# A transformer block on one core: the first stage put in another order, with wider dummy matmuls and earlier 256-column FFN blocks

## The chip, the core and the metric

The kernel runs on one core of a Trainium2 chip. The metric is the device time of one execution in microseconds (us). The core has a matrix engine (TensorE, PE in the profile; its weight loads are shown as PEld), a vector engine (DVE), a scalar engine (ACT), a general engine (POOL) and a queue engine (SP), which here issues nearly all DMA transfers. Each engine works through its own instructions in order and waits on semaphores for the others.

## The reference

The input x has 2048 rows of 448 columns, in bf16. It is normalized row by row. Two branches read the normalized rows: a linear attention with 16 heads of width 28 and a two-layer FFN of width 1792. Their results are added to x.

```python
xn  = layernorm(x)
q, k, v = split(xn @ wqkv)                     # 16 heads, width 28
pq, pk  = q @ w_phi, k @ w_phi                 # per head, 28x28
phi(p)  = concat(softmax(p), softmax(-p))      # width 56
num = phi(pq) @ (phi(pk).T @ v)
den = phi(pq) @ sum_s phi(pk) + 1e-6
A   = (num / den) @ wo
B   = silu(xn @ w1) @ w2
out = x + A + B
```

## The kernel before

The rows are worked on in 8 pairs of 128-row tiles. The kernel records every operation with the tiles that it reads and writes, an assumed duration and a priority, and `_Prog.schedule` then lays them out, engine by engine, with a planner of its own. The planner assumes when each load lands: SP issues one load every 550 ns, the bytes flow at up to 290 GB/s (150 GB/s for a transfer into 64 partitions, marked `half`), and a landing follows 1.7 us later. The order found is fixed at build time; semaphores then make each engine wait for what it needs. So the planner's figures decide the order and nothing else.

The work falls into stages:

- *First stage.* SP loads x pair by pair and w1 in column blocks. Dummy matmuls on a zeroed tile `zz` (L545, named "warm") fill PE until the first transposes. `ln_pair(p)` takes the row statistics on DVE (L611, L615), the power -0.5 on POOL (`rstd`, L622), and writes the normalized rows `xn_sb` (L635, on DVE; for pairs 4 to 7 the second tile on POOL). `ln_tr` brings them to column-major order in `xnT`: for pairs 0 to 3 by seven PE transposes (L504) and a copy out of PSUM ("eviction", on ACT for pair 0 at L650, on DVE for the others at L652), for pairs 4 to 7 by a transposing DMA (L556).
- `ffn1_chunk(p0, npair, fa, fb)` multiplies `npair` pairs with the feature tiles `fa` to `fb` of w1 (14 in all), 128 x npair columns to a matmul, and ACT applies SiLU into `hT`. Two PSUM units of two banks each are used in turn. The contraction of 448 goes as 7 steps of 64 rows on both halves of the array, so each weight must lie in both halves of the partitions: `load_main` and `load_tail` load it once, and `swap` copies it across (ACT L511 or DVE L576, one half each).
- `fold()` multiplies the transposed query and key weights `wT` (brought by eight transposing DMAs, L597, "wT_dt") with the per-head matrix of `w_phi` and writes the folded weights, key ones first, into `W_sb`, which lies in the tile `ar`; they are swapped too, and so are the value weights (columns `VO` to `WC`).
- *Key stage.* `k_macro(p)` projects keys and values of a pair, ACT takes the exponentials (L511), DVE copies the values (L773) and forms row sums `Sk` (L778) and reciprocals `Rk` (L780), and POOL multiplies (`phik`, L781). `k_acc` accumulates the key-value product on PE, `q_group` projects the queries.
- *Last stage.* FFN1 of pairs 4 to 7, the query side, FFN2 with w2, the output projection with wo, and the stores. `late_loads` brings w2 and wo; they wait for the exponentials of a pair (the key "early").

The order of recording in the first stage is this (the priorities are equal, so it also breaks ties):

```python
        ln_pair(0)
        swap(w1_sb, 0, 256, ("act", "act"))
        swap(w1_sb, 256, 512, ("act", "act"))
        ffn1_chunk(0, 1, 0, 4)
        ln_pair(1)
        swap(w1_sb, 512, 1024, ("act", "dve"))
        ffn1_chunk(0, 1, 4, 8)
        ffn1_chunk(1, 1, 0, 8)
```

Feature tiles 8 to 13 follow later for pairs 0 to 3 together, 512 columns to a matmul.

Of the kernel before, what the change touches and what calls it, by code (L numbers as in the profile page):

```python
# [144 lines left out]
class _Prog:  # L145
# [72 lines left out]
    def schedule(self):  # L218
# [28 lines left out]
        plan = {}  # L247
        loads = {e: [[o.id, o.nbytes, 0.0] for o in ops if o.is_dma and o.eng == e and not o.deps] for e in ("sp", "act")}
        for e, t0, per in (("sp", -100.0, 550.0), ("act", 1500.0, 600.0)):
            for i, q in enumerate(loads[e]):  # L250
                q[2] = t0 + per * (i + 1)
        now = 0.0
        while loads["sp"] or loads["act"]:
            live = [e for e in ("sp", "act") if loads[e] and loads[e][0][2] <= now]
            nxt = [loads[e][0][2] for e in ("sp", "act") if loads[e] and loads[e][0][2] > now]
            if not live:
                now = min(nxt)
                continue
            cap = [150.0 if ops[loads[e][0][0]].half else 290.0 for e in live]
            rates = [min(c, 290.0 * c / sum(cap)) for c in cap]  # L260
            step = min(min(loads[e][0][1] / r for e, r in zip(live, rates)), min(nxt) - now if nxt else 1e18)
            now += step
            for e, r in zip(live, rates):
                q = loads[e][0]
                q[1] -= step * r
                if q[1] <= 1.0:
                    plan[q[0]] = now + 1700.0
                    loads[e].pop(0)
# [92 lines left out]
def bass_parallel_sum__linear_kernel_hedgehog__dense_activation_silu__prompt_kernel(  # L361
# [20 lines left out]
    with es:  # L382
        def sb(name, shape, dt):
            return es.enter_context(nc.sbuf_tensor(name, shape, dt))
# [153 lines left out]
        P.cur_prio = 0  # L538
        table_op = act(mtmp[:, 0:1], ones4[:, 0:1], ACTF.Silu, "table", table="silu")
        P.cur_prio = 3  # L540
        NWARM = 46
        zz = sb("zz", [128, 256], BF16)
        P.op("dve", 300, lambda e: e.memset(zz[:], 0.0), writes=[zz[:]], name="zz")
        for i in range(NWARM):
            mm(banks[5][:, 0:256], zz[:, 0:128], zz[:, 0:256], True, True, "warm")  # L545
            P.ops[-1].dur = 215.0 if i < 26 else 110.0
        P.cur_prio = 0

        def load(dst, src, nbytes, name, eng="sp", keys_r=(), half=False):
# [8 lines left out]
        def load_x(p0, p1, eng="sp"):  # L558
            load(x_sb[:, 2 * p0:2 * p1, :].rearrange("p (q t) d -> p q t d", t=2), xt[:, p0:p1], (p1 - p0) * 256 * D * 2, f"x{p0}", eng)
# [17 lines left out]

        load_x(0, 1)
        load_main(w1_sb, B_w1, 0, 256, 0, "w1_0")
        load_tail(w1_sb[:, 6], B_w1, 0, 1024, 0, "w1_0t", "act")  # L580
        load_x(1, 2)
        load_main(w1_sb, B_w1, 256, 512, 256, "w1_0b")
        load_x(2, 3)
        load_main(w1_sb, B_w1, 512, 1024, 512, "w1_1")
        load_x(3, 4)
        if not 1:
            load_main(wraw, A_wqkv, 0, 2 * D, 0, "wqk")
            load_tail(wraw[:, 3], A_wqkv, 0, 2 * D, 0, "wqkt")
        load(Wp[:], A_w_phi.rearrange("(g hl) d f -> (hl d) g f", g=G), H * DH * DH * 2, "wphi")
        load_main(w1_sb, B_w1, 1024, FF, 1024, "w1_2")  # L590
        load_tail(w1_sb[:, 6], B_w1, 1024, FF, 1024, "w1_2t")
        load_x(4, 6)
        load_x(6, 8)
        if 1:
            for a in (4, 5, 6, 7, 0, 1, 2, 3):
                dst, src = wT[:, a:a + 1, 0:D], A_wqkv[:, a * KP:a * KP + 128]
                P.dma(lambda e, dst=dst, src=src: e.dma_start_transpose(out=dst, in_=src), 2 * D * 128 * 2, writes=[dst],  # L597
                      name="wT_dt", dur=700.0)
        load_main(W_sb, A_wqkv, 2 * D, 3 * D, VO, "wv")
        load_tail(W_sb[:, 6], A_wqkv, 2 * D, 3 * D, VO, "wvt")  # L600

        def late_loads():
            load(w2_sb[:], B_w2.rearrange("(f p) d -> p f d", p=128), FF * D * 2, "w2", keys_r=("early",))
            for k in range(3):
                load(wo_sb[:, k, :], A_wo[128 * k:128 * k + 128, :], 128 * D * 2, "wo", keys_r=("early",))
            load_tail(wo_sb[:, 6], A_wo, 0, D, 0, "wot")

        BK_F = [4, 7]
        first_xn = []
        def ln_stats(t):  # L610
            o = P.op("dve", 630, lambda e: e.bn_stats(st6[:, t, :], x_sb[:, t, :]),  # L611
                     reads=[x_sb[:, t, :]], writes=[st6[:, t, :]], name="bnst")
            if t >= 2:
                o.odeps |= {q.id for q in first_xn}
            P.op("dve", 180, lambda e: e.bn_aggr(mv[:, t, :], st6[:, t, :]),  # L615
                 reads=[st6[:, t, :]], writes=[mv[:, t, :]], name="bnag")

# [23 lines left out]
        def ln_tr(p, bk):  # L641
            sl = p % NXN
            dstx = xnT[:, :, p, :]
            if p >= 4:
                transpose_dma(dstx, xn_sb[:, sl, :], "xnT_dt")
                return
            tp = bank16[bk][:, 0:896].rearrange("p (j c) -> p j c", j=KB)
            transpose_many([(tp[:, j, :], xn_sb[:, sl, 128 * j:128 * j + 128]) for j in range(KB)], "xnT_tr")
            if p == 0:
                act(dstx, tp, ACTF.Identity, "xnT_ev")  # L650
                return
            P.op("dve", d_dve(896, 2), lambda e: e.tensor_copy(dstx, tp), reads=[tp], writes=[dstx], name="xnT_ev")  # L652

        def ln_pair(p):
            t0, t1 = 2 * p, 2 * p + 1
# [18 lines left out]
        def ffn1_chunk(p0, npair, fa=0, fb=FT, late=False):  # L674
            n = npair * 128
            F = 512 // n
            for f0 in range(fa, fb, F):
                w = min(F, fb - f0)
                b0 = UNITS[unit_no[0] % len(UNITS)]
                unit_no[0] += 1  # L680
                for i in range(w):
                    mm_448([banks[b0 + h][:, i * n:(i + 1) * n] for h in range(2)],
                           lambda h, k, ft=f0 + i: w1_sb[:, k, ft * 128:ft * 128 + 128],
                           lambda h, k: xnT[:, k, p0:p0 + npair, :].rearrange("p a c -> p (a c)"),
                           i == 0, True, "ffn1_mm")
                src = psum[:, b0 * 512:(b0 + 2) * 512].rearrange("p (r c) -> p r c", r=2)[:, :, 0:w * n]
                if w == 1:
                    dst = hT(f0, f0 + 1, 0, 2, p0, p0 + npair).rearrange("p f r a c -> p (f r) (a c)")
                else:
                    src = src.rearrange("p r (f c) -> p r f c", f=w)  # L690
                    dst = hT(f0, f0 + w, 0, 2, p0, p0 + npair).rearrange("p f r a c -> p r f (a c)")
                o = act(dst, src, ACTF.Silu, "silu", table="silu")
                if late:
                    lates.append(o)
                    for q in exps:
                        if q.id not in o.deps:
                            o.odeps.add(q.id)
                else:
                    silus.append(o)
# [8 lines left out]
        def fold():  # L708
# [2 lines left out]
                bd4, Wp[:, :, None, :].broadcast_to([KP, G, 4, DH]),  # L711
                maskh[:, None, :, None].broadcast_to([KP, G, 4, DH]), ALU.mult),
                reads=[Wp[:], maskh[:]], writes=[BDphi[:]], name="bdphi")
            if 1:
                for a in (4, 0):
                    src, dst = wT[0:KP, a:a + 4, 384:448], wT[0:KP, a:a + 4, 448:512]
                    P.op("dve", 230, lambda e, dst=dst, src=src: e.tensor_copy(dst, src), reads=[src], writes=[dst], name="wT_dup")
            for a0 in range(0, 0 if 1 else 8, 4):
                tps = [bank16[b][0:KP].rearrange("p (a c) -> p a c", a=2) for b in BK_F]
                transpose_many([(tps[i // 2][:, i % 2, kt * 128:kt * 128 + 128], wraw[:, kt, (a0 + i) * KP:(a0 + i + 1) * KP])  # L720
                                for i in range(4) for kt in range(4)], "wT_tr")
                for i in range(2):
                    act(wT[0:KP, a0 + 2 * i:a0 + 2 * i + 2], tps[i], ACTF.Identity, "wT_ev")
            for qk in (1, 0):
                for k0 in range(0, 4, 2):
                    parts = []
# [14 lines left out]
        swap(w1_sb, 256, 512, ("act", "act"))  # L741
        ffn1_chunk(0, 1, 0, 4)
        ln_pair(1)
        swap(w1_sb, 512, 1024, ("act", "dve"))
        ffn1_chunk(0, 1, 4, 8)
        ffn1_chunk(1, 1, 0, 8)
        ln_pair(2)
        ln_pair(3)
        fold()
        ffn1_chunk(2, 1, 0, 8)  # L750
        ffn1_chunk(3, 1, 0, 8)
        ln_pair(4)
        swap(w1_sb, 1024, FF, ("act", "dve"))
        ln_pair(5)
        ffn1_chunk(0, 4, 8, FT)
        ln_pair(6)
        ln_pair(7)
        swap(W_sb, VO, WC, ("dve", "dve"))

        def k_unit(p, j, b0, name):  # L760
            mm_448([banks[b0 + t][:, 0:D] for t in range(2)], lambda h, k: xnT[:, k, p, :],
# [49 lines left out]
                 writes=[vaug[:, sl, :, :, DH]], name="vaug1")  # L811
        for p in range(NPAIR):
            k_macro(p)
            if p == 1:
                P.keyw["early"] = exps[-1].id
                late_loads()
            q_group(p // 4, p % 4)
            if p in (2, 4, 6):
                k_acc(p - 2, p)
# [275 lines left out]
```

## Time and profile before

| | |
|---|---|
| median of three runs | 162.54 us (161.03 to 163.39) |
| profiled execution: its time | 159.93 us |
| its span, first to last instruction | 158.2 us |
| granted TensorE clock | 1.000 |
| PE busy | 151.5 us (96%), 2687 matmuls |
| DVE, ACT, POOL busy | 101.4, 75.0, 65.0 us |
| DMA | 12.10 MB in 22905 packets |
| first real matmul, first key projection | 9.84 us, 38.62 us |

Busy time is summed over an engine's instructions. The chain that ended last goes back from the last instruction, at each step to whatever released it; a step named "issue" is time for which the profile shows nothing that was waited for. In a timeline row the first number is the start, the second the length of a group of instructions, then the engine, the line, the operation, out <- in with its shape, the count, and in brackets the idle time before it and what ended it.

### The profile page before, as it was taken

To read this page: it belongs to the slowest core of one execution; us is meant where nothing else is said; L and a number is where in the kernel's file an instruction comes from. 1 tells how busy PE (TensorE), PEld (TensorE's weight loads), DVE (VectorE), ACT (ScalarE), POOL (GpSimd) and SP (SyncE) were. 2 spreads that over 40 slices of the span, in tenths; PEclk is the share of its full clock that TensorE was granted. 3 is DMA by queue.
4 is the path that set the end of the run, shared out by engine and by line. 5 is a ranking of instruction groups with operands and counts; after the bars stand their busy time and mean duration, and the time that the engine had idled before them with its cause. 6 is when DMAs were issued, how large, how long until landed. Compare 5 with 4: busy or idle time off the path is not lost.

```text
span 158.2 us, 5909 instructions
## 1 busy us (share of the span) xinstructions
PE 151.5 (96%) x2687; PEld 97.1 (61%) x2687; DVE 101.4 (64%) x194; ACT 75.0 (47%) x81; POOL 65.0 (41%) x73
## 2 busy tenths in 40 slices
PE   7979699999999999999999999999999999999994
PEld 5777588644444645446778889755555555556553
DVE  5887579884478869688468796667985950022041
ACT  3689267876988878587775665830000000000000
POOL 5221209788046776767900533664166051000000
PEclk9999999999999999999999999999999999999999
DMA  4999883572207900000000023030440044041011
GB/s 120 263 328 261 152 109 94 62 62 58 58 4 198 298 1 6 4 0 4 6 4 4 4 58 62 12 50 4 116 117 6 4 116 116 4 116 58 4 58 58
DMA packets 22905, 12.10 MB, mean 77 GB/s; under 512 B 16096, under 2 KB 22752, under 8 KB 22880
## 3 DMA queue, kind: packets, MB, share of 16 engines
q1 hardware_dynamic: 22720, 11.47, 32.9%
q8 instruction: 21, 0.34, 1.0%
q10 hardware_dynamic: 160, 0.26, 0.6%
q14 instruction: 4, 0.03, 0.1%
HBM read 6.22 MB, written 1.84 MB: 51 GB/s over the span
## 4 chain that ended last, share of the span: by engine, by line
PE 89%; DMA 3%; issue 3%; ACT 2%; SPq 1%; DVE 0%
PE psum L486 85%; PE psum L479 4%; DMA w_sb<-in_B_w_dram 3%; ACT w_sb L511 1%; PE psum L504 1%; SPq L550 1%; ACT ar L511 1%; ACT xnT L511 1%; DVE out_sb L933 0%; ACT L511 0%
## 5 line engine op out<-in xcount | busy, mean ns | idle before, releaser
L486 PE MATMUL psum<-xnT,w_sb 64*128 64x128 bf16 (+2 forms) x924 | 46.0, 253 | 3.3 <-issue 2.2
L486 PEld LDWEIGHTS psum<-xnT,w_sb 64*128 64x128 bf16 x924 | 35.3, 94 | 11.9 <-issue 2.7
L511 ACT ACTIVATE ar<-psum 128x896 bf16<-128x896 f32 (+2 forms) x38 | 32.0, 880 | 10.7 <-PE psum L486 10.6
L889 POOL TENSOR_TENSOR scr<-scr 128x384 bf16<-128x384 f32 (+3 forms) x32 | 20.1, 659 | 31.5 <-DVE scr L884 20.6
L781 POOL TENSOR_TENSOR ar<-ar,Rk 128x1792 bf16<-128x1792 bf16 (+1 forms) x9 | 25.8, 2876 | 14.3 <-DVE Rk L780 12.0
L933 DVE TENSOR_TENSOR out_sb<-psum,x_sb 128x448 bf16<-128x448 f32 (+2 forms) x17 | 9.5, 593 | 23.7 <-PE psum L486 20.5
L486 PE MATMUL psum<-ar,xnT 64*128 64x448 bf16 x224 | 22.7, 349 | 0.0
L486 PE MATMUL psum<-w_sb,hT_lo 64*128 64x448 bf16 x224 | 22.3, 349 | 0.0
L511 ACT ACTIVATE eq<-psum 128x1024 bf16<-128x1024 f32 x16 | 15.5, 1025 | 6.1 <-PE psum L486 6.0
L511 ACT ACTIVATE hT_lo<-psum 128x1024 bf16<-128x1024 f32 x14 | 14.3, 1022 | 7.9 <-PE psum L486 7.9
L778 DVE TENSOR_REDUCE Sk<-ar 128x64 f32<-128x1792 bf16 (+1 forms) x9 | 16.2, 1804 | 2.5 <-ACT ar L511 2.5
L486 PEld LDWEIGHTS psum<-ar,xnT 64*128 64x128 bf16 x224 | 10.8, 94 | 10.6 <-DVE ar L773 0.4
L884 DVE TENSOR_TENSOR scr<-psum,Gq 128x896 f32<-128x896 f32 x16 | 16.9, 1087 | 0.4
L486 PE MATMUL psum<-w_sb,ar 64*128 64x448 bf16 x168 | 16.6, 349 | 0.0
L486 PEld LDWEIGHTS psum<-w_sb,hT_lo 64*128 64x128 bf16 x224 | 10.5, 94 | 9.4
L622 POOL TENSOR_TENSOR rstd<-ve,neghalf 128x2 f32<-128x2 f32 (+1 forms) x9 | 7.1, 792 | 18.6 <-DVE ve L620 16.4
L486 PE MATMUL psum<-xnT,ar 64*128 64x512 bf16 x112 | 13.4, 376 | 0.0
L773 DVE CAST ar<-psum 128x896 bf16<-128x896 f32 x8 | 8.6, 1070 | 7.4 <-PE psum L486 7.4
L486 PEld LDWEIGHTS psum<-w_sb,ar 64*128 64x128 bf16 x168 | 8.4, 94 | 7.4
L486 PE MATMUL psum<-wo_sb,scr 64*128 64x448 bf16 (+2 forms) x119 | 11.9, 338 | 0.0
L635 POOL TENSOR_SCALAR xn_sb<-x_sb,mv,rstd 128x192 bf16<-128x192 bf16 (+1 forms) x8 | 9.9, 1241 | 0.7 <-POOL rstd L622 0.4
L611 DVE BATCH_NORM_STATS2 st<-x_sb 128x6 f32<-128x448 bf16 x16 | 9.6, 612 | 0.1
(51 smaller groups left out, 122.2 us busy)
## 6 DMA issues: line engine op xcount, KB each, us to landing
w_sb<-in_B_w_dram SPq DMA_DIRECT2D x1, 1568.0 KB, 7.8
out_dram<-out_sb SPq DMA_DIRECT2D x7, 224.0 KB, 2.2
x_sb<-in_A_x_dram SPq DMA_DIRECT2D x4, 224.0 KB, 5.0
x_sb<-in_A_x_dram SPq DMA_DIRECT2D x2, 448.0 KB, 8.0
w_sb<-in_B_w_dram SPq DMA_DIRECT2D x1, 576.0 KB, 7.0
w_sb<-in_B_w_dram SPq DMA_DIRECT2D x2, 192.0 KB, 3.8
w_sb<-in_B_w_dram SPq DMA_DIRECT2D x1, 384.0 KB, 5.9
ar<-in_A_wqkv_dram SPq DMA_DIRECT2D x1, 336.0 KB, 3.5
```

Source lines behind the costliest of these rows:

```text
L479: lambda e: e.matmul(dst, lhsT, rhs, start=start, stop=stop, skip_group_check=True),
L486: r = e.matmul(dst, lhsT, rhs, start=start, stop=stop, skip_group_check=True)
L511: return P.op("act", d_act(_cols(src)), lambda e: e.activation(dst, src, func, scale=scale), reads=[src], writes=[dst], table=table, name= ...
L611: o = P.op("dve", 630, lambda e: e.bn_stats(st6[:, t, :], x_sb[:, t, :]), reads=[x_sb[:, t, :]], writes=[st6[:, t, :]], name="bnst")
L622: P.op("pool", 580, lambda e: e.tensor_tensor(r2, v2, nh, ALU.pow), reads=[v2, nh], writes=[r2], name="rstd")
L635: o = P.op("pool" if pool else "dve", 150 + _cols(xs) * 1.6 if pool else 120 + _cols(xs) * 0.6, lambda e, xn=xn, xs=xs: e.tensor_scalar(xn ...
L773: P.op("dve", d_dve(896), lambda e: e.tensor_copy(dstv, vb), reads=[vb], writes=[dstv], name="v_ev")
L778: P.op("dve", d_dve(896 * n), lambda e, S3=S3, E3=E3: e.tensor_reduce(S3, E3, AXL.X, ALU.add), reads=[E3], writes=[S3], name="Sk")
L781: P.op("pool", d_pool(896 * n, 1.77), lambda e, E3=E3, R3=R3, n=n: e.tensor_tensor(E3, E3, R3[:, :, None].broadcast_to([128, 32 * n, DH]), ...
L884: P.op("dve", d_dve(896), lambda e, dsto=dsto, Us=Us, Gs=Gs: e.tensor_tensor(dsto, Us, Gs[:, :, :, :, None].broadcast_to([128, 2, 2, 8, DH ...
L889: P.op("pool", d_pool(_cols(a0), 2.26), lambda e, dst=dst, a0=a0, a1=a1: e.tensor_tensor(dst, a0, a1, ALU.add), reads=[a0, a1], writes=[ds ...
L933: P.op("dve", d_dve(c1 - c0), lambda e: e.tensor_tensor(dst, ob, xs, ALU.add), reads=[ob, xs], writes=[dst], name="out_ev")
```

## The change

- The 31 + 15 dummies of 256 columns become 18 of 512 columns and 10 of 256; `zz` grows to 512 columns and is zeroed in two steps. In the order found, 18 stand before the first transposes, 9 after them and 1 later.
- Pair 0 is evicted by DVE (L652's form) and no longer by ACT. DVE's statistics of the second tile follow the first tile's instead of standing beside them; later statistics are held behind the evictions of pairs 0 and 1.
- w1 comes in another order: columns 512 to 1024, the last 64 rows of columns 512 to 1792, and columns 1024 to 1408 and 1408 to 1792 now stand ahead of x of pairs 2 and 3. The two loads on ACT's queue carry 512 instead of 1024 columns each. The swaps are cut in the same way.
- Feature tiles 8 to 13 are computed for pairs 0 and 1 right after the first block, and for pairs 2 and 3 among the fold's matmuls, with 256 columns each.
- The eight transposing loads of the query and key weights stand ahead of x of pairs 4 to 7, and so behind 12 transfers instead of 13.
- The value weights' swap is recorded in `fold()`, and in the order found stands between the key swaps and the query swaps; the statistics of pair 4 stand ahead of these on DVE.
- w2 is loaded in parts of 4, 3, 4 and 3 feature tiles, released by the exponentials of pairs 1 to 4, and wo by those of pair 5.
- The planner's assumed rates change (310 and 190 GB/s, 1.5 us for a transposing load, one stop of 0.9 us).

```diff
-            cap = [150.0 if ops[loads[e][0][0]].half else 290.0 for e in live]
-            rates = [min(c, 290.0 * c / sum(cap)) for c in cap]
+            cap = [190.0 if ops[loads[e][0][0]].half or ops[loads[e][0][0]].name == "wT_dt" else 310.0 for e in live]
+            rates = [min(c, 310.0 * c / sum(cap)) for c in cap]
...
-        for i in range(NWARM):
-            mm(banks[5][:, 0:256], zz[:, 0:128], zz[:, 0:256], True, True, "warm")
+        for n, rows, cols, dur in ((8, 128, 512, 430.0), (10, 128, 512, 215.0), (10, 128, 256, 109.0)):
+            for i in range(n):
+                mm(banks[5][0:rows, 0:cols], zz[:, 0:rows], zz[:, 0:cols], True, True, "warm")
...
         load_main(w1_sb, B_w1, 0, 256, 0, "w1_0")
-        load_tail(w1_sb[:, 6], B_w1, 0, 1024, 0, "w1_0t", "act")
+        load_tail(w1_sb[:, 6], B_w1, 0, 512, 0, "w1_0t", "act")
         load_x(1, 2)
         load_main(w1_sb, B_w1, 256, 512, 256, "w1_0b")
+        load_main(w1_sb, B_w1, 512, 1024, 512, "w1_1")
+        load_tail(w1_sb[:, 6], B_w1, 512, FF, 512, "w1_1t")
+        load_main(w1_sb, B_w1, 1024, 1408, 1024, "w1_2a")
+        load_main(w1_sb, B_w1, 1408, FF, 1408, "w1_2b")
         load_x(2, 3)
-        load_main(w1_sb, B_w1, 512, 1024, 512, "w1_1")
         load_x(3, 4)
         load(Wp[:], ...)
-        load_main(w1_sb, B_w1, 1024, FF, 1024, "w1_2")
-        load_tail(w1_sb[:, 6], B_w1, 1024, FF, 1024, "w1_2t")
-        load_x(4, 6)
-        load_x(6, 8)
             for a in (4, 5, 6, 7, 0, 1, 2, 3):
                 ...
+        load_x(4, 6)
+        load_x(6, 8)
...
-            if p == 0:
-                act(dstx, tp, ACTF.Identity, "xnT_ev")
-                return
-            P.op("dve", d_dve(896, 2), lambda e: e.tensor_copy(dstx, tp), reads=[tp], writes=[dstx], name="xnT_ev")
+            o = P.op("dve", d_dve(896, 2), lambda e: e.tensor_copy(dstx, tp), reads=[tp], writes=[dstx], name="xnT_ev")
...
-        swap(w1_sb, 512, 1024, ("act", "dve"))
+        swap(w1_sb, 512, 768, ("act", "dve"))
+        swap(w1_sb, 768, 1024, ("act", "dve"))
         ffn1_chunk(0, 1, 4, 8)
+        swap(w1_sb, 1024, 1408, ("act", "dve"))
+        swap(w1_sb, 1408, FF, ("act", "dve"))
+        ffn1_chunk(0, 2, 8, FT)
+        ln_pair(2)
         ffn1_chunk(1, 1, 0, 8)
-        ln_pair(2)
         ln_pair(3)
         fold()
         ffn1_chunk(2, 1, 0, 8)
+        ln_pair(4)
+        ffn1_chunk(2, 2, 8, FT)
         ffn1_chunk(3, 1, 0, 8)
-        ln_pair(4)
-        swap(w1_sb, 1024, FF, ("act", "dve"))
         ln_pair(5)
-        ffn1_chunk(0, 4, 8, FT)
         ln_pair(6)
         ln_pair(7)
-        swap(W_sb, VO, WC, ("dve", "dve"))
```

## The prediction

> **What bounds the kernel now.** I read the page first (engines, slices), then the chain that ended last in order of time, then the timeline of the first 55 us. TensorE (PE) is busy 96% of the span, so the question is only where it is not. The chain in order of time (start us, length us, what) answers that:
>
> ```profile
> 9.84 2.52 PE psum L486 x84
> ...
> 13.96 1.50 PE psum L486 x49
> 15.46 1.79 issue
> ...
> 21.43 0.36 issue
> ...
> 26.55 51.29 PE psum L486 x969
> ...
> 80.58 69.89 PE psum L486 x1096
> ```
>
> From 26.55 us on the chain is PE work but for 2.7 us around 79 us, in which PE itself idles only 0.3. So a change to the first stage pays only by starting the first real matmul (9.84) earlier, by taking out the idle 1.79 and 0.36 us, or by bringing the first key projection forward; and the gain lasts only if the later stage can follow. The timeline shows what sets 9.84:
>
> ```profile
> 1.10 5.89 PE L479 MATMUL psum<-zz 128*128 128x256 bf16 x31 [1.10 <-DVE zz L543]
> 6.94 0.56 PE L504 MATMUL psum<-ident,xn_sb 128*128 128x128 bf16 x7
> 7.14 1.71 ACT L511 ACTIVATE w_sb<-w_sb 64x768 bf16<-64x768 bf16 x2 [1.38 <-DMA w_sb<-in_B_w_dram]
> 7.34 1.69 PE L479 MATMUL psum<-zz 128*128 128x256 bf16 x14
> 8.87 0.92 ACT L511 ACTIVATE xnT<-psum 128x896 bf16<-128x896 bf16 x1
> ```
>
> The transposes of pair 0 end at 7.50, but their eviction waits on ACT behind two weight swaps until 8.87: 1.4 us lost.
>
> The "issue" gaps stand after 221, 348 and 475 matmuls (the third, 26.51 to 26.55, is tiny), counted along the timeline: 127 apart. Each matmul has a weight load, so that is 254 instructions; the page's queue q8 moved 0.34 MB in 21 packets for 5374 PE instructions, 64 bytes each, 256 to a packet. I read the gaps as PE waiting for its next packet of instructions while data fills the DMA engines (in the window 14 to 16 us they are busy 1.90 of 2.00 us). If a packet is asked for one packet ahead, the first took 6.1 us (asked about 11.1, there at 17.25), the next two 4.5 and 4.8.
>
> **The change, part by part.** *Dummies.* The 14 later dummies run 0.109 us apart ((1.69 - 0.27)/13); the first 31 average 0.187 ((5.89 - 0.27)/30), so about 21 ran at twice 0.109, until some 5.8 us, though the granted clock reads 1.00 throughout. Eighteen dummies of 512 columns, started near 1.3 (more to zero first), then take ten at 0.436 and eight at 0.218: they end at 7.45. LayerNorm's xn ends about 7.2 instead of 6.87, as DVE now asks for the second tile's rstd after the first xn (one xn of 0.3). So the dummies cost some 0.25.
>
> The Trainium skill, page "TensorE: Matmul & The Clock Gate", Part 1, says that the warm-up is a budget of time, about 3.4 us, and not a number of matmuls, so wider dummies cannot warm the array sooner. The trace has 4.7 us. By the page's 3.4 the 18 would end at 6.9 (an estimate) and the transposes would wait for xn at 7.2, 0.25 us better than my sum.
>
> *Eviction of pair 0 on DVE.* Transposes 7.45 to 8.05, a DVE copy of 0.63 (the L652 group's mean is 626 ns), first matmul at 8.85, when the nine narrow dummies (0.98) also end. 9.84 - 8.85 = **1.0 gained**. ACT's half tail loads and w1's second 256 columns do not stand in the way: the latter landed at 7.12 and now have 128 KB less ahead.
>
> *Early 256-column blocks.* Feature tiles 8 to 13 of pairs 0 and 1 follow the first block, those of pairs 2 and 3 stand among the fold matmuls. Work: 84 matmuls of 512 columns at 0.110 become 168 of 256 at 0.056.
>
> ```profile
> 31.06 7.73 PE L486 MATMUL psum<-xnT,w_sb 64*128 64x512 bf16 x70
> 84.88 5.51 PE L486 MATMUL psum<-xnT,w_sb 64*128 64x256 bf16 x98
> ```
>
> That is 9.28 against 9.45: 0.2 lost. New waits: pair 1's eviction stands on DVE behind a swap of 384 columns (1152 elements, 0.55 by the 0.62 for 1344), so PE, done at 12.75, goes on at 13.2: 0.45. On ACT two such swaps (1.16 each, between 0.84 for 768 and 1.48 for 1536) stand between the first two SiLUs, so tile 10 finds its bank free at 15.1, not 14.8: 0.3. The instruction gaps mostly go: the 221st matmul now falls on the 67th of the 84 wide ones, near 17.4, while its packet, asked for at 10.65, is there by 15.2 to 16.8. For the next two I keep 0.3 (bounds 0 and 2.15). The loads these blocks need are early: by the windows of 2 us 2.18 MB had moved by 10 us and 2.85 MB by 12; in the new order w1's last part completes 2.29 MB and x of pair 2 2.52 MB, so they land near 11.1 and 11.7 (0.7 for the landing), and x is used at 13.6.
>
> Sum of the stage: 28.8 us from 9.84 to the first key matmul at 38.62, less 2.15 idle, plus 0.45, 0.3, 0.2, 0.3 gives 27.9, from 8.85: first key matmul at 36.75, **1.9 earlier**.
>
> *Query and key weights ahead of x of pairs 4 to 7; value swaps ahead of query swaps.* On SP the x loads of pairs 4 to 7 move behind the eight transposing loads:
>
> ```profile
> 7.01 1.12 SPq L550 DMA_DIRECT2D x_sb<-in_A_x_dram  x2
> 8.17 13.14 SPq L597 DMA_TRANSPOSE eq<-in_A_wqkv_dram  x8
> 21.36 1.76 SPq L550 DMA_DIRECT2D ar<-in_A_wqkv_dram  x3
> ```
>
> SP reaches the transposes after 12 issues instead of 13, near 7.2, so x of pair 4 is issued at 20.3 instead of 7.0 and lands near 24.2 (as the value weights issued at 21.36 took 3.5). On DVE its statistics now stand ahead of the key and value swaps, then the query swaps (waiting for the last fold, about 32.1), then statistics and norms of pairs 5 to 7. POOL's rstd (0.8) and half of xn (2.4) for three pairs follow one another from about 34.7: 9.7 us, ended near 44.7. Before, this chain was done at 39.2 and POOL then stood idle:
>
> ```profile
> 36.78 2.44 POOL L635 TENSOR_SCALAR xn_sb<-x_sb,mv,rstd 128x192 bf16<-128x192 bf16 x2 [0.18 <-POOL rstd L622]
> 45.68 3.21 POOL L781 TENSOR_TENSOR ar<-ar,Rk 128x1792 bf16<-128x1792 bf16 x1 [6.45 <-DVE Rk L780]
> 50.08 3.22 POOL L781 TENSOR_TENSOR ar<-ar,Rk 128x1792 bf16<-128x1792 bf16 x1 [1.19 <-DVE Rk L780]
> 53.84 1.23 PE L486 MATMUL psum<-ar 64*56 64x58 bf16 x128
> ```
>
> Those 6.45 us are the cover of the move, and they are used up. The first row sum Sk now stands behind the xn of pair 7, from 42.9: Rk at 45.5, the two phik products 45.6 to 48.8 and 49.2 to 52.4, and PE's first key-value block cannot start before 52.7. By PE alone it would start at 53.84 - 1.9 = 51.95. So up to 0.75 of the gain is lost; bounds 0 (the chain of xn runs a microsecond quicker) and 1.9 (all). I take 0.6.
>
> *w2 in four parts.* The 1568 KB load ran from 47.4 to 55.2 under a PE that stayed busy, and w2 is first read past 100 us. The parts wait on ACT one step after another; behind them on SP stand only wo and the later transposes, first needed at 91. Nothing, either way; without that cover the last part would cost its quarter, 2 us.
>
> **Sum.** 1.9 - 0.6 = 1.3 on the profiled execution: 159.93 (span 158.2) becomes 158.6. The median shown is 162.54, 2.6 above it. As PE is solid from 26.55 on, I put that excess into the loads and instruction packets of the first stage, which the change relieves: between 0 and 2.6 of it goes, I take 1.3. Gain 2.6, **159.9 us**.
>
> **Rivals.** *All of it arrives:* the chain through POOL hides and the whole excess goes: 1.9 + 2.6 = 4.5, 158.0. For it: DVE needs only 3.7 us a step against PE's 4.2, so it catches up. Against: POOL's 2.4 us per half xn is steady.
> *x of pair 4 lands late (slower than before):* DVE stands at its statistics, and behind it the key, value and query swaps, so the folded weights, the key projection and the whole chain above slip. Slack: 24.2 to about 25.45, as the first key swap waits for the fold until 27.3. Each us past that costs one. It equals the gain when x lands at 28.05 and makes 2% at 31.3. If the eight transposes each take the longest 2.2 us (17.7 instead of 13.1) and x the 7.0 it took before, it lands at 31.9: 159.9 + 6.4 = 166.3. Against: the ring is nearly empty by then.
> *It does not do what it says:* the cold clock lasts longer or the DVE eviction waits on a late swap, and the 256-column blocks wait for SiLU: start and gaps unchanged, 0.2 left, 162.3.
>
> **How the numbers follow.** Forecast 0.54 (own range 158.2 to 161.8; 0.26 of it below 159.3), all of it arrives 0.16, late x 0.24 (0.05 of it still within 2%), nothing 0.06. Two per cent is 3.25 us, about what a measurement of this kernel can tell from no change. Faster 0.26 + 0.16 = 0.42, within 0.28 + 0.06 + 0.05 = 0.39, slower 0.19. The range runs from 157.0 (most of the second case) to 165.5 (part of the third).
>
> **What would show it.** First real matmul at 8.6 to 9.1 and first key matmul at 36 to 37.5; no issue gap over 0.5 before 26 us; POOL idle under 1.5 us before its first phik; first key-value block between 52 and 53.5. Wrong if DVE waits on x of pair 4 past 26 us, if an issue gap of over a microsecond stands inside the wide blocks, or if PE idles in the key stage by more than 1.5 us.

## The result, and the profile after

The changed kernel takes 158.85 us (median of 20 runs, 157.81 to 160.85); 20 runs of the kernel before, taken beside them, have 161.44 us (159.15 to 163.39). The ratio is 0.9879, 95% interval [0.9853, 0.9904]: 1.9 us gained, measured clearly, but less than 2%. Ratios here and below leave out runs more than 1.5% above the fastest of their kernel, medians keep all runs, and so the two medians lie 2.6 us apart. The profiled execution took 159.7 us (span 157.9, granted clock 1.000), against 159.93 (158.2) before.

So in the two profiled executions almost nothing separates the kernels (0.2 us), and in the usual runs 2 us do. Both facts need explaining. The timeline of the changed kernel, PE and DVE, its first 36 us (start, length, engine, line, operation, out <- in, count, idle before it and what ended that):

```profile
1.25 6.83 PE L483 MATMUL psum<-zz 128*128 128x512 bf16 x18 [1.25 <-DVE zz L547]
...
7.92 0.55 PE L508 MATMUL psum<-ident,xn_sb 128*128 128x128 bf16 x7
...
8.51 0.62 DVE L661 COPY xnT<-psum 128x896 bf16<-128x896 bf16 x1 [0.69 <-PE psum L508]
...
9.40 2.91 PE L490 MATMUL psum<-xnT,w_sb 64*128 64x128 bf16 x98
...
13.63 4.85 PE L490 MATMUL psum<-xnT,w_sb 64*128 64x256 bf16 x84 [0.22 <-DVE xnT L661]
...
35.71 2.81 PE L490 MATMUL psum<-ar,xnT 64*128 64x448 bf16 x28
```

The first real matmul starts at 9.40 (9.84 before), and the first key matmul at 35.71 (38.62 before): 2.9 us earlier. Between them PE is idle for 0.22 of 26.31 us; before it was idle for 2.20 of 28.78. The groups of PE instructions in that stretch (count | busy us, mean ns | idle before), first of the kernel before:

```profile
L486 PE MATMUL psum<-xnT,w_sb 64*128 64x128 bf16 x448 | 14.4, 216 | 3.0 <-issue 2.2 <-ACT xnT L511 0.8
L486 PE MATMUL psum<-xnT,w_sb 64*128 64x512 bf16 x84 | 9.4, 376 | 0.0
```

and of the changed one:

```profile
L490 PE MATMUL psum<-xnT,w_sb 64*128 64x128 bf16 x448 | 13.5, 216 | 0.0
L490 PE MATMUL psum<-xnT,w_sb 64*128 64x256 bf16 x168 | 9.9, 270 | 0.2 <-DVE xnT L661 0.2
```

The "issue" idle of 2.2 us is gone. By busy time the wide blocks cost 0.5 more in halves, and the narrow ones 0.9 less. Most of the latter is the gaps again: the profile counts a narrow matmul as busy for 216 ns, though in a row they start 0.03 us apart (126 in 3.72 us in the second profile of the kernel before). So at each of the three gaps of the kernel before PE stood still for some 0.19 us longer than the idle entry says, 0.56 in all. For the other 0.3 the trace gives no reason.

The packet that PE needs after its 221st matmul ends on the instruction queue at 14.97 us here and at 15.62 before, and PE now starts that matmul at 17.3 instead of 15.2 us, as many ahead of it are wider. A packet that ends earlier and a PE that comes later both shorten the wait; no run has the wide blocks alone, so their shares stay open.

The key stage, DVE, PE and POOL in the same timeline, shows where the 2.9 us went:

```profile
27.07 0.63 DVE L617 BATCH_NORM_STATS2 st<-x_sb 128x6 f32<-128x448 bf16 x1 [3.56 <-DMA x_sb<-in_A_x_dram]
...
39.19 0.70 DVE L645 TENSOR_SCALAR xn_sb<-x_sb,mv,rstd 128x384 bf16<-128x384 bf16 x2 [0.38 <-POOL rstd L632]
...
40.15 1.08 DVE L793 CAST ar<-psum 128x896 bf16<-128x896 f32 x1
...
41.29 2.82 PE L490 MATMUL psum<-ar,xnT 64*128 64x448 bf16 x28 [1.26 <-DVE ar L793]
...
45.57 3.21 POOL L801 TENSOR_TENSOR ar<-ar,Rk 128x1792 bf16<-128x1792 bf16 x1 [0.91 <-DVE Rk L800]
...
46.49 2.82 PE L490 MATMUL psum<-ar,xnT 64*128 64x448 bf16 x28 [0.87 <-DVE ar L793]
...
53.40 1.39 PE L490 MATMUL psum<-ar 64*56 64x58 bf16 x128
```

PE waits twice for a value copy (L793), and its first key-value block starts at 53.40, where it started at 53.84 before. From that block on both kernels need 104.4 to 104.5 us. The chain that ended last says what stood ahead of the second copy (start, length, what):

```profile
39.24 2.16 POOL xn_sb L645 x2
...
41.54 0.72 POOL rstd L632
...
42.36 0.61 DVE xn_sb L645 x2
42.97 1.93 DVE Sk L798
...
44.93 0.55 DVE Rk L800
45.48 0.96 DVE ar L793
...
46.49 33.57 PE psum L490 x820
```

Before, this chain was PE alone from 26.55 to 77.84; now it runs through POOL's normalization and DVE's queue.

One number is used for the key stage from here on: the stretch from the first key matmul to the first key-value block, less the 15.22 us (53.84 - 38.62) that PE needs when it waits for nothing. This **loss** is 2.47 us in the changed kernel (53.40 - 35.71 - 15.22). Both kernels and the twelve experiments in one table ("gap" is the longest issue idle of PE between the first real matmul and the first key matmul). The columns up to the span are of one profiled execution, the last two of all timed runs; for "w2 in four" (162.35 us) and "eviction alone" (162.50 us) the profiled execution is one of the longest:

| run | first real matmul | gap | first key | loss | span | median, us | ratio |
|---|---|---|---|---|---|---|---|
| before | 9.84 | 1.79 | 38.62 | 0 | 158.2 | 161.44 | 1 |
| after | 9.40 | 0 | 35.71 | 2.47 | 157.9 | 158.85 | 0.9879 [0.9853, 0.9904] |
| before, again | 10.37 | 1.68 | 38.47 | 0 | 158.0 | | |
| x ahead, in after | 8.69 | 0.92 | 36.80 | 1.01 | 158.1 | 160.02 | 0.9863 [0.9792, 0.9934] |
| DVE order, in after | 8.90 | 0 | 35.41 | 0.72 | 156.0 | 157.69 | 0.9762 [0.9696, 0.9828] |
| fewer dummies, in before | 10.35 | 2.68 | 40.43 | 0 | 161.1 | | |
| w2 in one piece, in after | 8.69 | 0.24 | 35.51 | 1.76 | 158.5 | 160.28 | 0.9953 [0.9920, 0.9987] |
| w2 in four, in before | 10.16 | 3.05 | 41.05 | 0 | 160.6 | 161.04 | 0.9980 [0.9943, 1.0018] |
| eviction alone, in before | 9.16 | 3.37 | 41.20 | 0 | 160.8 | 158.85 | 0.9839 [0.9789, 0.9888] |
| DVE order further, fewer dummies | 8.68 | 0 | 35.36 | 2.46 | 158.1 | 161.04 | 0.9990 [0.9950, 1.0030] |
| DVE order, fewer dummies | 8.70 | 0 | 35.13 | 0.72 | 156.0 | 157.84 | 0.9854 [0.9805, 0.9903] |
| x behind, in before | 9.96 | 0.36 | 42.81 | 0 | 162.5 | 164.55 | 1.0282 [1.0230, 1.0333] |
| eviction alone, second profile | 9.04 | 1.04 | 37.29 | 0 | 156.9 | | |
| DVE order, x of pair 4 earlier | 9.34 | 0 | 35.65 | 0.46 | 155.9 | 157.32 | 0.9799 [0.9739, 0.9858] |

### The profile page after: what moved, and what is told of

Read it like the earlier page. It is cut to its first block, busy times and chain, and to the rows that moved or that the text cites. A ratio compares the mean times of both kernels' runs of the same rounds, so it can differ in the third digit from the quotient of the medians.

```text
span 157.9 us, 6053 instructions
## 1 busy us (share of the span) xinstructions
PE 151.8 (96%) x2753; PEld 98.6 (62%) x2753; DVE 102.7 (65%) x198; ACT 74.2 (47%) x82; POOL 64.2 (41%) x73
## 4 chain that ended last, share of the span: by engine, by line
PE 67%; DVE 5%; POOL 2%; issue 0%; DVEq 0%
PE psum L490 63%; PE psum L483 3%; POOL xn_sb L645 1%; DVE Sk L798 1%; DVE KVZ L855 1%; DVE kvs L847 1%; DVE kvs L848 1%; DVE ar L793 1%; POOL rstd L632 0%; DVE xn_sb L645 0%; DVE Rk L800 0%; DVE out_sb L953 0%; DVEq L1055 0%
## 5 line engine op out<-in xcount | busy, mean ns | idle before, releaser
L490 PE MATMUL psum<-xnT,w_sb 64*128 64x256 bf16 (+1 forms) x1008 | 45.6, 246 | 0.2 <-DVE xnT L661 0.2
L490 PEld LDWEIGHTS psum<-xnT,w_sb 64*128 64x128 bf16 x1008 | 39.1, 94 | 4.8 <-DVE xnT L661 0.4
L515 ACT ACTIVATE eq<-psum 128x1024 bf16<-128x1024 f32 x16 | 15.5, 1024 | 6.2 <-PE psum L490 6.1
L793 DVE CAST ar<-psum 128x896 bf16<-128x896 f32 x8 | 8.6, 1069 | 4.1 <-PE psum L490 4.1
```

What stands on the lines that cost most here:

```text
L490: r = e.matmul(dst, lhsT, rhs, start=start, stop=stop, skip_group_check=True)
L515: return P.op("act", d_act(_cols(src)), lambda e: e.activation(dst, src, func, scale=scale), reads=[src], writes=[dst], table=table, name= ...
L793: P.op("dve", d_dve(896), lambda e: e.tensor_copy(dstv, vb), reads=[vb], writes=[dstv], name="v_ev")
```

## Experiments on the gap

**The kernel before, unchanged, once more.** Is its profile, below its median, an exception?

> The kernel before, unchanged, profiled a second time. Its first profile took 159.9 us, its median is 161.4. Theory: the excess of a usual run lies in the first stage, as longer waits for instruction packets or loads: with a time of 161 to 162 the first key matmul should then stand at 39.5 to 41 us instead of 38.62, and everything after it be as long as in the first profile (119.6 us from there to the end of the span). Rival: the excess lies outside the first stage (key stage or the end): first key matmul at 38.6 again, with PE idle elsewhere.

Measured: 159.79 us, span 158.0; gap 1.68 after the same 221 matmuls, first key matmul at 38.47. Two profiled runs of before, 159.93 and 159.79, lie below its usual 161.4. So the gap's place is fixed, and what makes the usual run longer is not in these two traces.

**Fourteen dummies fewer in the kernel before.** If the gap is a packet of 256 PE instructions that has not come, it follows the count of instructions, not the work.

```diff
+        warm = [i for i in order["pe"] if ops[i].name == "warm"]
+        gone = set(warm[31:45])
+        order["pe"] = [i for i in order["pe"] if i not in gone]
```

> The kernel before without the 14 dummies between the transposes of pair 0 and the first real matmul; nothing else is changed. Theory (PE waits for its next packet of instructions): the long gap stands again after about 221 matmuls in all, so 14 real matmuls later than before (after 183 instead of 169 FFN and transpose matmuls from the first one on), and is 1 to 3 us long. Rival (PE waits there for a weight or a SiLU): the gap stays in front of the same real matmul, after 207 in all.

Measured: 162.84 us. The gap stands 14 matmuls later, behind the last of the 56 and the seven transposes:

```profile
16.07 0.56 PE L504 MATMUL psum<-ident,xn_sb 128*128 128x128 bf16 x7
19.32 5.09 PE L486 MATMUL psum<-xnT,w_sb 64*128 64x128 bf16 x126 [2.68 <-issue]
```

So it follows the count of instructions, as a packet does. And something more is seen: the 126 matmuls behind it take 5.09 us where the second profile of before has 3.72 for the same 126. After an idle time of 2.68 us PE ran at half rate for a while: the granted clock is 0.50 from 20 to 22 us, and 0.989 in the mean of the run. The length of the idle time alone does not decide this. In the same run PE idled 2.87 us ahead of its first real matmul, and the 84 matmuls behind that took 2.52 us, as in the kernel before.

**x of pairs 4 to 7 behind the transposing loads, in the kernel before.** This moves 0.9 MB out of the way of the packet and changes nothing else in the program.

```diff
+        xs = [i for i in sp if ops[i].name in ("x4", "x6")]
+        rest = [i for i in sp if i not in xs]
+        at = max(k for k, i in enumerate(rest) if ops[i].name == "wT_dt") + 1
+        order["sp"] = rest[:at] + xs + rest[at:]
```

> The kernel before with one thing changed: SP's loads of x of pairs 4 to 7 (0.9 MB) issued behind the eight transposing loads, as in the changed kernel. Theory: the packet of PE instructions needed at the 222nd matmul comes behind these bytes, so the issue gap of 1.7 to 3.4 us near 15.5 us goes down to 0 to 0.7 us, and PE does not fall to half rate behind it; but x of pair 4 lands near 27 and VectorE, GpSimd and the key stage run late as in the changed kernel: first key matmul 36 to 37.5, first key-value block 53 to 54, ratio 0.985 to 0.995. Rival (the gap is set by how fast PE eats its instructions, narrow ones as before, and not by the loads): the gap stays over 1.2 us, and with the late x the ratio is 1.0 to 1.01.

Measured: the gap is 0.35 at its old place, as the theory said (the next one, after 348 matmuls, stays at 0.36), but the time is 164.55 us, ratio 1.0282 [1.0230, 1.0333], outside both forecasts. PE and DVE of its timeline:

```profile
15.92 0.39 PE L486 MATMUL psum<-xnT,w_sb 64*128 64x128 bf16 x7 [0.35 <-issue]
...
22.85 0.63 DVE L611 BATCH_NORM_STATS2 st<-x_sb 128x6 f32<-128x448 bf16 x1 [4.78 <-DMA x_sb<-in_A_x_dram]
...
24.53 0.93 PE L504 MATMUL psum<-ident,xn_sb 128*128 128x128 bf16 x7 [3.52 <-DVE xn_sb L635]
...
26.14 3.17 PE L486 MATMUL psum<-xnT,w_sb 64*128 64x128 bf16 x56
```

The statistics of pair 4 stand on DVE ahead of the norm of pair 3, so PE waits 3.52 us for x, and then needs 3.17 us for 56 matmuls that took 1.74 before (granted clock 0.50 from 24 to 28 us). The theory of the gap held; my forecast of the time did not, because I had left DVE's order out. It also shows why the changed kernel had to change that order along with the loads.

**x of pairs 4 to 7 ahead of the transposing loads, in the changed kernel.** The reverse step.

```diff
+        at = min(k for k, i in enumerate(rest) if ops[i].name == "wT_dt")
+        order["sp"] = rest[:at] + xs + rest[at:]
```

> The kernel after, with only SP's order changed: the two loads of x of pairs 4 to 7 stand ahead of the eight transposing loads again. Theory (late x starts the chain through DVE and POOL late, and PE then waits for the value copy in the key stage): x of pair 4 lands by 17 us instead of 27.0, DVE's idle 3.6 us before its statistics goes, PE's wait for the copy of the first values falls from 1.26 us to under 0.5 and the second from 0.9; ratio to before near 0.980 against 0.988. Rival (the swaps of the query weights, which wait for the last fold, start the chain anyway): x lands early, but the waits in the key stage stay within 0.4 us and the ratio stays 0.986 to 0.990.

Measured: 160.02 us. x lands at 15.0 and 17.7, and the packet is late again, inside the wide block:

```profile
15.15 2.25 PE L490 MATMUL psum<-xnT,w_sb 64*128 64x256 bf16 x37 [0.21 <-ACT hT_lo L515]
18.31 1.26 PE L490 MATMUL psum<-xnT,w_sb 64*128 64x256 bf16 x19 [0.92 <-issue]
```

The loss of the key stage falls to 1.01, but 1.1 us later start of the key stage takes it back. Wide matmuls alone do not remove the gap; the bytes ahead of the packet count.

**Eviction of pair 0 on DVE, alone, in the kernel before.**

```diff
-                act(dstx, tp, ACTF.Identity, "xnT_ev")
+                P.op("dve", ..., lambda e: e.tensor_copy(dstx, tp), ...)   # behind the fourth bnag
```

> The kernel before with only the eviction of pair 0 moved from ACT to DVE, behind the statistics of pair 1. First real matmul near 9.1 instead of 9.84 to 10.4. Theory (the next packet of instructions comes when the data in front of it is through, whenever it is asked for): the gap after 221 matmuls grows by what the start gains, the first key matmul stays within 0.3 us of 38.6, ratio 0.997 to 1.003. Rival (the packet comes a fixed time after it is asked for): all of the start arrives, first key matmul near 37.9, ratio 0.993 to 0.997.

Measured: 158.85 us over six runs, four at 158.15 to 158.94 and two at 161.73 and 162.50; ratio 0.9839 [0.9789, 0.9888], by the four. Neither theory had so much. The profiled run is the one of 162.50, so a second profile of the same program was taken:

> The kernel before with the eviction of pair 0 on VectorE alone, once more, for a profile: in time it gained 1.6%, where the packet theory had 0.3% at most. Theory now: with the first real matmul at 9.2 instead of 9.8 to 10.4, the packet gap comes 0.7 earlier and is as much longer, but the key stage starts no later, and what gained is something behind it: the profile should show a first key matmul at 37.5 to 38.0 and a span of 156 to 157.5. Rival: the gain is in the gap itself, which is under 1.2 us in the usual run, so PE's clock stays up: gap under 1.2, first key matmul at 37.0 to 37.5. Third: nothing of the kind, span 158 or more, and the gain of the timed runs is the one chip's.

Measured: 158.62 us, span 156.9. PE's timeline in the two profiles of this one program, the run of 162.50 first:

```profile
9.16 1.93 PE L486 MATMUL psum<-xnT,w_sb 64*128 64x128 bf16 x56
...
19.04 0.40 PE L486 MATMUL psum<-xnT,w_sb 64*128 64x128 bf16 x8 [3.37 <-issue]
...
19.87 5.32 PE L486 MATMUL psum<-xnT,w_sb 64*128 64x128 bf16 x126
```

```profile
9.04 1.74 PE L486 MATMUL psum<-xnT,w_sb 64*128 64x128 bf16 x56
...
16.20 0.40 PE L486 MATMUL psum<-xnT,w_sb 64*128 64x128 bf16 x8 [1.04 <-issue]
...
17.02 4.01 PE L486 MATMUL psum<-xnT,w_sb 64*128 64x128 bf16 x126
```

The same instructions, and the gap is 3.37 or 1.04 us; with the long one PE then runs at half rate. The first key matmul is at 41.20 or 37.29, 3.9 us apart, which is the whole difference of the runs. In the DMA view the instruction queue moves one packet between 14.5 and 15.7 us in the kernel before, 13.6 and 14.8 in the second profile here, 16.3 and 17.6 in the first, and PE goes on some 1.5 us behind it each time (17.25, 16.20, 19.04). The second expectation's rival came true: gap under 1.2, first key 37.0 to 37.5. My error was to take the packet's arrival as given. In the run with the short gap it comes 1 us earlier than before, about as much as PE began earlier (9.04 against 9.84), so there an earlier start is not eaten by the gap. In the run with the long gap the loads ahead of the packet are late too: x of pair 4 lands at 15.05 instead of 14.36 us. What slows them is not shown.

## Experiments on the key stage

**DVE's order in the changed kernel.** The first value copy goes ahead of the norm of pair 6, the first row sum and reciprocal ahead of the norm of pair 7.

```diff
+        # was: xn6 xn6 bnag bnag ve v_ev xn7 xn7 Sk Rk
+        s = dv[v0 - 5:v0 + 5]
+        order["dve"] = dv[:v0 - 5] + [s[5], s[0], s[1], s[2], s[3], s[4], s[8], s[9], s[6], s[7]] + dv[v0 + 5:]
```

> The kernel after, with only DVE's order changed: the copy of the first values stands ahead of the norm of pair 6, and the first row sum and reciprocal ahead of the norm of pair 7. Theory (the gain of the first stage is lost because these wait in DVE's queue behind norms that wait for POOL): PE's waits for the value copies in the key stage (1.26 and 0.87 us) fall under 0.3 each, the first key-value block starts near 51.5 instead of 53.4 with the first key matmul unmoved at 35.7, and the ratio goes from 0.988 to 0.976 to 0.980. Rival (the key stage is bound by POOL's products or by PE itself): the first key-value block still starts after 52.8 and the ratio stays within 0.985 to 0.990.

Measured: 157.69 us, ratio 0.9762 [0.9696, 0.9828], span 156.0. Its timeline:

```profile
38.26 1.09 DVE L793 CAST ar<-psum 128x896 bf16<-128x896 f32 x1 [0.47 <-PE psum L490]
...
39.57 2.81 PE L490 MATMUL psum<-ar,xnT 64*128 64x448 bf16 x28
...
43.56 3.21 POOL L801 TENSOR_TENSOR ar<-ar,Rk 128x1792 bf16<-128x1792 bf16 x1
...
44.43 2.82 PE L490 MATMUL psum<-ar,xnT 64*128 64x448 bf16 x28 [0.54 <-DVE ar L793]
```

The first copy now waits for PE and not the other way round; the loss falls from 2.47 to 0.72. The second wait, forecast under 0.3, is still 0.54. So 1.75 of the 2.47 us were the order of ten instructions on DVE.

**The second copy moved too, and four of the 18 dummies dropped.**

```diff
+        order["dve"] = dv[:v0 - 5] + [s[5], s[0], s[1], s[2], s[3], s[4], s[8], s[9], s[10], s[6], s[7]] + dv[v0 + 6:]
+        gone = set(warm[14:18])
```

> The kernel after with DVE's order changed as in the earlier run (first value copy ahead of the norm of pair 6, first row sum and reciprocal ahead of that of pair 7), now also the second value copy ahead of the norm of pair 7, and four of the 18 wide dummies left out. Theory: PE's remaining wait for the second value copy (0.54 us) goes, the first real matmul comes at 8.6 to 9.2 instead of 9.4, and both reach the end: ratio 0.966 to 0.973. Rival (POOL's products bind next, and the start is lost at the first block behind w1's later columns): ratio 0.974 to 0.978, as without the two.

Measured: 161.04 us, ratio 0.9990 [0.9950, 1.0030]: nothing left of the gain. Its timeline:

```profile
43.23 3.21 POOL L801 TENSOR_TENSOR ar<-ar,Rk 128x1792 bf16<-128x1792 bf16 x1
43.53 3.24 DVE L645 TENSOR_SCALAR xn_sb<-x_sb,mv,rstd 128x384 bf16<-128x384 bf16 x2
...
46.69 2.00 DVE L798 TENSOR_REDUCE Sk<-ar 128x64 f32<-128x1792 bf16 x1
...
50.29 2.82 PE L490 MATMUL psum<-ar,xnT 64*128 64x448 bf16 x28 [2.28 <-DVE ar L793]
```

The norm of pair 7 now runs beside POOL's product and takes 3.24 us instead of 0.74; it ends at 46.77, 0.3 behind the product, and everything behind it on DVE is late. The profiled run took 159.87 us; 7 of the 12 runs show a granted clock of 0.989, with a median of 161.36, and this profile does not show what happens in those. To separate this from the dropped dummies, the next run keeps the dummies out and the second copy in its place:

> The changed kernel with VectorE's order of the experiment on it (first value copy ahead of the norm of pair 6, first row sum and reciprocal ahead of the norm of pair 7) and with 4 of the 18 wide dummies dropped, the second value copy left where it was. Theory: what the version with the second value copy moved too lost, it lost because the norm of pair 7 then ran beside GpSimd's first product of 3.2 us and took 3.2 us instead of 0.7. Here that norm runs ahead of the product: 0.7 us, first real matmul near 8.7, first key-value block at or below 51.4, ratio to the kernel before 0.968 to 0.977. Rival: the fewer dummies are what cost (PE's clock gated for longer, or the instruction packets late): ratio 0.985 to 1.0, with a gap of PE in the first 35 us.

Measured: 157.84 us, ratio 0.9854 [0.9805, 0.9903], first real matmul at 8.70, loss 0.72. Its ratio misses the expected 0.968 to 0.977 and lies at the edge of the rival's range, but the gap that the rival asks for is not there, and span, loss and time are those of the run with DVE's order alone (156.0, 0.72, 157.69); the kernel before was at 160.62 beside it and at 161.57 beside the other. So the collision of norm and product was the cause of the lost 1.74 us in the key stage, and the fewer dummies neither cost nor bring anything that shows.

**x of pair 4 behind the sixth transposing load, with DVE's order.** How much of the loss is the late x?

```diff
+        xs = [i for i in sp if ops[i].name == "x4"]
+        at = [k for k, i in enumerate(rest) if ops[i].name == "wT_dt"][5] + 1
```

> The changed kernel with VectorE's order of the earlier experiment (first value copy ahead of the norm of pair 6, first row sum ahead of the norm of pair 7) and one SP load moved: x of pairs 4 and 5 goes behind the sixth of the eight transposing loads instead of behind the eighth. Theory: with x of pair 4 landed near 21 instead of 27.0, VectorE's statistics stand no longer in the way of the key and value copies, which then wait only for the fold (start near 27.4 instead of 28.9), the chain of rstd and norms through GpSimd runs 1 to 1.5 us earlier, and what is left of PE's waits on the value copies (0.17 and 0.54) goes; 0.45 MB in the middle of the transposes lets the instruction packet through: no issue gap over 0.3 before 35 us. First key matmul 35 to 35.6, first key-value block 50.4 to 50.9, median 156.7 to 157.5. Rival: the packet gap comes back with the load (0.5 to 1.2 us between 17 and 25 us), as with the loads ahead of all eight: first key 36 to 36.8, median 158 to 159.

Measured: 157.32 us, ratio 0.9799 [0.9739, 0.9858], first key-value block at 51.33 instead of the expected 50.4 to 50.9. x lands at 21.3, no gap comes back, and the key copies start at 26.26, but the loss only falls from 0.72 to 0.46:

```profile
44.42 2.82 PE L490 MATMUL psum<-ar,xnT 64*128 64x448 bf16 x28 [0.29 <-DVE ar L793]
```

With DVE's order set right, the late x is worth a quarter of a microsecond, by one profile of each. This version, the DVE order alone and the DVE order with fewer dummies all have lower medians than both kernels (157.3 to 157.8); the runs do not tell them apart.

## Experiments on w2

**One piece in the changed kernel, four in the kernel before.**

```diff
-            a, b = ((0, 4), (4, 7), (7, 11), (11, FT), (0, 0))[part]
+            a, b = ((0, FT), (0, 0))[part]
```

> The kernel after with w2 loaded in one piece, released by the exponentials of pair 1, and wo behind it, as before; only SP's order differs. Theory (w2 hidden either way): ratio to before 0.985 to 0.991, as the kernel after. Rival (the unprofiled runs of before are 1.6 us above its profile because the one large load delays PE's instruction packets): ratio 0.993 to 1.000, and a new PE gap between 50 and 65 us.

> The kernel before with only w2 in four parts and wo behind them. Theory (hidden either way): ratio 0.997 to 1.003. Rival (the large load delays packets in the unprofiled runs): 0.988 to 0.993, which would be nearly the whole gain of the change.

Measured: in one piece in the changed kernel 160.28 us, ratio 0.9953 [0.9920, 0.9987], against 0.9879 [0.9853, 0.9904] with four; in four pieces in the kernel before 161.04 us, ratio 0.9980 [0.9943, 1.0018], nothing. The timeline of the first:

```profile
52.49 1.19 PE L490 MATMUL psum<-ar 64*56 64x58 bf16 x123
...
54.95 0.22 PE L490 MATMUL psum<-ar 64*56 64x58 bf16 x5 [1.27 <-issue]
```

Another packet gap. In the windows from 48 to 52 us this load keeps all DMA engines busy (347 to 358 GB/s), and the packet needed after the 123rd of these tiny matmuls comes behind it. In the kernel before the same load ran in one piece without a gap: there PE came to its first key-value block after 66 matmuls fewer (792 against 858, counted along the timelines), and the same packet was needed only at 61 us, after the load. So the split belongs to the 256-column blocks; alone it is worth nothing. With four parts, gaps of 0.17 to 0.42 us are left at this place in four other profiles.

## Why the prediction was right, and where it was not

The forecast was 159.9 us by the first of the cases; measured are 158.85. Step by step:

- **Dummies.** They were to cost 0.25; in the profiled run they cost 0.85 (transposes at 7.92, xn ready at 7.07). In the four other profiles with the same 18 dummies the transposes start at 7.22, 7.22, 7.43 and 7.87, so the cost runs from nothing to 0.85: the 18 take 5.59, 5.83, 6.33, 6.78 and 6.83 us. A cold one lasts 0.43 and a warm one 0.22, so some 8 to 14 of them were cold, 3.3 to 5.8 us. The first real matmul was forecast at 8.85; the five profiles have 8.69, 8.69, 8.90, 9.34 and 9.40. The size was right for the middle, and the profile that was taken lies at the late end. On the Trainium skill's rule weighed there ("TensorE: Matmul & The Clock Gate", Part 1): its 3.4 us is the early end of what was measured; the page also says that the cold phase differs from run to run, and here it does.
- **Eviction on DVE.** Right: the copy took 0.62, the start gained 0.44 in this profile, 0.50 in one other and 0.94 to 1.15 in three, against a forecast of 1.0.
- **256-column blocks.** By busy time the halves cost 0.5 (9.9 - 9.4), not 0.2; set against the 0.3 of the narrow matmuls for which no reason shows, 0.2 is left. The wait for pair 1's eviction was 0.22, not 0.45; the wait of 0.3 for the SiLU did not stop PE.
- **Instruction packets.** Right, and shown: no issue gap before the first key matmul where 0.3 was kept. The gap follows the instruction count, shrinks when the x loads move away, and comes back when they return. The size was short: I took out the 2.15 of the idle entries, and with the 0.56 above PE had stood still for 2.75.
- **First key matmul.** 35.71 against the forecast 36.75. The gaps and waits gave 0.8 more than I kept, and the narrow matmuls 0.9 that I had not counted (0.56 of it the gaps); the late start and the halves took 0.85 back.
- **Key stage.** This is the step that failed: a loss of 0.6 was forecast (bounds 0 and 1.9), 2.47 was measured. The chain through POOL was right nearly to the tenth (norms ended at 44.66, forecast 44.7; products at 45.57 and 49.01, forecast 45.6 and 49.2), but I let PE come to it unhindered, "by PE alone", and asked only what the products wait for. PE itself waits for the value copies, which free its PSUM banks and stand on DVE behind norms that wait for POOL. Moving the first copy and the first row sum, with nothing else, brought 1.75 of it back. The first key-value block at 53.40 lies inside the 52 to 53.5 that I named, but by luck: the first key matmul came 1.0 earlier than forecast, and the loss was 1.9 larger. Of the three signs of being wrong two came: DVE waited for x past 26 us (to 27.07), and PE idled 2.13 us in the key stage, over 1.5.
- **x of pair 4.** Forecast to land at 24.2, it landed at 27.04 here, and at 24.25 to 25.85 in four other profiles of the same load order. I gave it the 3.5 us of a smaller load (20.3 and 3.5 make 23.8, not 24.2); from issue to landing it took 6.36 us here and 3.89 to 5.67 there. With 24.25 and the old DVE order the loss is still 1.76. The rival of a late x had its sign: DVE waited 3.56 us, past the 25.45 that it named, but the FFN work covered that, and the key projection was not late. Its mechanism decides in the kernel before, where PE had no such cover: 2.8% slower.
- **w2.** "Nothing, either way" held for the kernel before and not for the changed one, where the split saves a gap of 1.27.
- **The excess of the median over the profile.** 2.6 us over three runs, 1.5 over 20; I let half of 2.6 go. All of it went: the changed kernel's median lies 0.85 below its profiled run. On the profiled run I was 1.1 too low (158.6 against 159.7), on the excess 2.15 too high (+1.3 against -0.85). The two errors leave 1.05 of 159.9, and the gain by the medians, 2.6, is the one forecast; that they offset each other is luck. That the excess was packet gaps of changing length fits the two profiles of one program above, and the clock: of 57 runs of the kernel before beside the experiments, 26 have a mean granted clock of 0.98 to 0.99 and a median of 161.8 us, the other 31 have 1.00 and a median of 160.6; all 20 of the changed kernel have 1.00. For the unprofiled runs of before it is argued and not shown.

Where the gain came from is thus told apart in the profiles: the start and the packet gap bring some 3 us to the key stage, of which 2.5 are lost there, 1.75 by DVE's order. In time the whole change (ratio 0.9879) gains no more than the eviction alone does in four of its six runs (0.9839). What the rest of the change seems to add is that the long gap stays away: none of the changed kernel's 20 runs has a granted clock under 1.00, and the other two runs of the eviction alone have 0.989.

## What to carry to other kernels

Where an engine shows "issue" idle at a fixed count of instructions, look at what the DMA engines carry at that moment: here the idle time shrank from 1.79 to 0.35 us when 0.9 MB of loads went behind the packet, came back with 0.92 when they went ahead of it, and a large load elsewhere brought one of 1.27 us. When a step is moved on one engine, go through every instruction behind it in that engine's queue and ask which of them frees a buffer for the engine that sets the end, not only which feeds the longest chain. And profile a kernel more than once before sizing a wait: one program showed the same wait at 1.04 and at 3.37 us.

## What the runs showed of the hardware

- A packet of PE instructions comes late behind data transfers: 1.04 and 3.37 us of idle PE in two executions of one program. The Trainium skill ("Runtime: NRT & Kernel Launch", Instruction fetch mechanics) has the packets of 256 instructions, and the traces agree; it calls the cost of crossing one mostly hidden, and here it is not.
- After idle times of 2.68, 3.05, 3.37 and 3.52 us PE ran at half rate for a few microseconds (126 matmuls in 5.09, 5.32 and 5.32 us, 56 in 3.17), and the granted clock in windows of 2 us fell to between 0.50 and 0.59. After 2.28 it did not (28 in 2.82, as always), nor after 2.87 (84 in 2.52), so the idle time alone does not set it.
- DVE's norm of 0.74 us took 3.24 while POOL's product of 3.21 ran. The Trainium skill ("SBUF — State Buffer", Who interferes with whom) has this as an exclusive lock on ports that VectorE and GpSimd share, held for a whole instruction; the norm's end 0.3 us behind the product's agrees.
